# A fused attention and expert kernel: the work beside the attention scores is put into other units of each pair of heads

## The chip, the cores and the metric

The kernel runs on one core of a Trainium2 chip. The metric is the device time of one execution in microseconds (us), lower is better. The core has engines that run side by side, each through its own list of instructions in order: TensorE (PE in the profile, its weight loads PEld), VectorE (DVE), ScalarE (ACT), GpSimd (POOL), and SyncE (SP), which here only issues transfers (DMAs). An instruction that waits holds up everything behind it on its engine.

## The reference, cut to what matters

Three layers follow one another. The first is attention on 2 batches, 8 heads, 768 positions and 64 features per head, in which a query sees only the keys that fall into the same hash bucket; the second sends 1536 tokens to 8 experts; the third is a gated feed-forward layer with three matrices of 512 x 1536, 512 x 1536 and 1536 x 512.

```python
q_bits = (np.einsum('bhsd,dk->bhsk', q, proj) > 0)      # 6 bits a position; k_bits alike
mask = q_bucket[:, :, :, None] == k_bucket[:, :, None, :]
scores = np.where(mask, scale * np.matmul(q, k.transpose(0, 1, 3, 2)), -1e9)
attn = softmax(scores)
out = np.matmul(attn, v)
...                                                     # the experts: token to expert by greedy choice
x = silu(xn @ w_gate) * (xn @ w_val) @ w_out            # the third layer
```

The matrices of the third layer arrive as 64-bit floats, shown to the kernel as 64-bit integers (the "wide weights"). They are needed as 32-bit floats only hundreds of microseconds later, and are converted while the attention runs.

## The kernel before, in words

The attention takes the heads in 8 pairs (two heads of one batch). A pair has 12 **units**: 6 blocks of 128 queries by 2 heads. So there are 96 units, and the place of a unit in its pair runs from 0 to 11. In unit u the program writes down, in this order: the exponentials of unit u+1 (`expo`, L350, ScalarE); the six transposes of unit u (`transp`, L361, TensorE), whose two halves are copied out of the accumulator memory (PSUM), one by VectorE (L365) and one by ScalarE (L363), or both by ScalarE at places 0, 4 and 8; the scores of unit u+2 (`scores`, L336 and L339, TensorE) and their row minimum and exponent scale on VectorE (L341 to L343); the combination of a finished block (`comb`, L395, and L420 on VectorE) in even units, the reciprocals (L404, L405, VectorE) in odd ones; a part of the product with the values (`pv`, L380, TensorE); and then what is in `fill` for this unit. The transposes, the combination and the preparation share three PSUM buffers called m, in turn: a transpose waits until the buffer of three uses ago has been copied out.

Two kinds of work are in `fill`, put there by tables of unit numbers.

**Preparation of the next pair.** For the keys and then the queries, in two halves each, `prep_t` transposes on TensorE (L278), copies to SBUF on ScalarE (L282, L284) and splits into a high and a low part on GpSimd (L285, L286). After the second half `prep_d` issues six transfers on SyncE that stack the parts (L310 to L312). Two `prep_p` steps compute hash bits (six matmuls L294, then L297 on VectorE into the tile sg), and `prep_s` issues four transfers of sg (L320) into the stacked operands s_k and s_q. Then `load_pair` issues the loads of the pair after that (L98). `SLOTS` gives the places: keys at -1 and 0, queries at 1 and 3, `prep_p` at 5 and 6, and with the second of these `prep_s`. The first matmul of the next pair that needs what `prep_s` moves is L339 in unit 10 of the pair.

**Conversion of the wide weights.** 36 pieces of 128 x 512. For each, `conv_load` (L242, SyncE) is due five units ahead of `conv`, and `conv_store` (L263, SyncE) three units behind it. `conv` is one ScalarE instruction (L250), two VectorE instructions from SBUF to SBUF (L253, L254) and four GpSimd instructions (L255 to L258). The unit of piece n is 5 + 12n/5, rounded down, so that a pair has five pieces, spread over all its units (places 0, 2, 5, 7 and 9 in most pairs). A piece's load buffer is one of three, its sg buffer one of two, its ha buffer one of four.

Within a unit the preparation stands ahead of the conversion, and a piece's store ahead of the load of a later piece. The order of every engine is fixed by this writing order (`manual_schedule`): nothing is moved afterwards.

Of the kernel before, what the change touches and what calls it, by code (L numbers as in the profile page):

```python
# [23 lines left out]
BIG = 2.0 ** 30  # L24
ACT_EVAC = 1
SLOTS1 = (0, 0, 4, 5, 5, 6)
CONV = 5
SLOTS = (-1, 0, 1, 3, 5, 6)
WSTEP = (4, 7, 9, 10, 10, 13, 15, 16)
POOL_LO = (0, 1, 4, 5, 7)  # L30
DVE_HI = (0, 4)
# [15 lines left out]
def lsh_attention__moe__swiglu_kernel(ctx, tc, q, k, v, proj, m_wg, m_w1, m_w2,  # L47
# [8 lines left out]
    TPB = S // 128  # L56
# [5 lines left out]
    NPAIR = B * HP  # L62
# [164 lines left out]
    convs = []  # L227
    for src, dst in ((f_wg, wg_d), (f_wv, wv_d), (f_wo, wo_d)):
        n = src.shape[0] * src.shape[1] // (128 * 512)
# [281 lines left out]
    def at(u, f, *a):  # L511
        fill.setdefault(u, []).append((f, a))

    for p in range(1, NPAIR):
        u0 = (p - 1) * TPB * 2
        slots = iter(SLOTS if p > 1 else SLOTS1)
        for nm in "kq":
            for half in range(2):
                n = u0 + next(slots)
                at(n, prep_t, p, nm, half)  # L520
            at(n, prep_d, p, nm)
        for half in range(2):
            n = u0 + next(slots)
            at(n, prep_p, p, half)
        at(n, prep_s, p)
        if p + 1 < NPAIR:
            at(n + 1, load_pair, p + 1)
    for n in range(len(convs)):
        u = CONV + n * 12 // 5
        at(u - 5, conv_load, n)  # L530
        at(u, conv, n)
        at(u + 3, conv_store, n)
    for i in range(8):
# [779 lines left out]
```

## Time and profile before

| | |
|---|---|
| median of 3 runs | 816.4 us (815.01 to 816.46) |
| the profiled execution's own time | 814.53 us |
| its span, first to last instruction | 812.7 us |
| TensorE busy in the span | 761.3 us (94%) |
| VectorE, ScalarE, GpSimd busy in the span | 513.7, 398.0, 328.6 us |
| mean granted TensorE clock | 0.967 of full speed |
| the 96 units | from 22.1 us to 298.9 us |

Times in the rows are counted from the start of the span. "Busy" of TensorE includes matmuls that overlap one another, so 94% does not say that only 6% can be saved. The attention is read pair by pair: a stretch runs from the first transpose (L361) of a pair's unit 0 to that of the next pair. A bracket at the end of a timeline row is the idle time of that engine ahead of the instruction and what ended it. Behind the attention come the choice of the experts, the experts and the feed-forward layer, which the change does not touch.

### The profile page before, as it was taken

What the parts mean: (1) busy time and instruction counts of PE and PEld (TensorE: products, weight loads), DVE (VectorE), ACT (ScalarE), POOL (GpSimd) and SP (SyncE); (2) the same over time, 40 slices, a digit from 0 to 9 for tenths busy, and PEclk for the clock granted to TensorE, in tenths of its full rate; (3) what the DMA queues carried; (4) which work ended last, traced back from release to release, by engine and by line L of the source; (5) the groups of instructions that cost most, each with busy time, mean ns of one, the idle gap of its engine ahead of it and who ended that gap; (6) DMA issues with size and microseconds to landing.
All of it is one profiled execution on the core that took longest, in us unless ns stands there. A gap on an engine that the chain in (4) does not pass through costs nothing.

```text
span 812.7 us, 14759 instructions
## 1 busy us (share of the span) xinstructions
PE 761.3 (94%) x5317; PEld 685.2 (84%) x5317; DVE 513.7 (63%) x1342; ACT 398.0 (49%) x863; POOL 328.6 (40%) x309
## 2 busy tenths in 40 slices
PE   7999999999989983698999999999999999999997
PEld 3788777787878863498999999999999999999996
DVE  7788786889878878467787887766422332233222
ACT  3677765676766762265676776644211221121111
POOL 3278786877868720586767660000100010001001
PEclk8999999999999995699999999999999999999999
DMA  3578897989879612377777834363200110001001
GB/s 79 175 206 217 258 248 208 271 253 278 213 233 268 192 34 78 96 226 226 244 255 241 261 102 156 117 195 117 78 1 1 40 39 1 1 1 40 1 1 39
DMA packets 89770, 115.58 MB, mean 142 GB/s; under 512 B 22124, under 2 KB 68188, under 8 KB 89692
## 3 DMA queue, kind: packets, MB, share of 16 engines
q1 hardware_dynamic: 87612, 108.28, 44.8%
q0 software_dynamic: 1920, 6.29, 2.1%
q8 instruction: 44, 0.72, 0.4%
q14 instruction: 34, 0.28, 0.1%
q10 hardware_dynamic: 160, 0.00, 0.0%
HBM read 77.62 MB, written 18.87 MB: 119 GB/s over the span
## 4 chain that ended last, share of the span: by engine, by line
PE 37%; issue 18%; POOL 1%; DVE 1%; ACT 1%; POOLq 0%; ACTq 0%; DVEq 0%
PE pg L1194 6%; PE pv L1194 6%; PE py L1029 6%; PE po L1222 6%; PE ph L1005 6%; PE py L1031 3%; PE ph L1007 3%; POOL out_dram L1230 1%; PE ph L983 1%; PE py L1101 0%; DVE wl L218 0%; PE px L1061 0%; PE px L1084 0%; ACT bt L1015 0%; DVE yn L1091 0%
## 5 line engine op out<-in xcount | busy, mean ns | idle before, releaser
L1230 POOL DMA_INDIRECT out_dram<-ot,oi x12 | 11.7, 974 | 307.8 <-DVE ot L1228 306.2
L350 ACT ACTIVATE pr<-sc,rs 128x768 f32<-128x768 f32 x96 | 94.9, 989 | 50.4 <-DVE rs L343 31.6
L341 DVE TENSOR_REDUCE rs<-sc 128x1 f32<-128x768 f32 x96 | 91.5, 953 | 34.7 <-PE sc L339 34.2
L218 POOL TENSOR_TENSOR wl<-wr,wh 128x1024 fp32r<-128x1024 f32 x39 | 95.0, 2446 | 44.0 <-PE ph L983 20.9
L1203 DVE TENSOR_TENSOR a<-sg,pg 128x384 f32<-128x384 f32 x48 | 26.6, 553 | 103.1 <-ACT sg L1201 103.1
L361 PE MATMUL m<-ident,pr 128*128 128x128 f32 x576 | 83.4, 281 | 3.1 <-ACT pt L363 2.5
L380 PE MATMUL xo<-pt,ld_v 128*64 128x128 f32 x1128 | 82.9, 282 | 0.0
L1005 PE MATMUL ph<-xg,wh 128*128 128x384 f32 x256 | 75.3, 363 | 3.8 <-DVE ht L1022 3.1
L1029 PE MATMUL py<-ht,wh 128*128 128x384 f32 x256 | 76.7, 364 | 0.0
L361 PEld LDWEIGHTS m<-ident,pr 128*128 128x128 f32 x576 | 63.8, 141 | 15.1 <-issue 7.4
L380 PEld LDWEIGHTS xo<-pt,ld_v 128*64 128x64 f32 x1128 | 60.0, 137 | 18.6 <-issue 11.9
L1201 ACT ACTIVATE sg<-pg 128x384 f32<-128x384 f32 x48 | 23.5, 490 | 105.8 <-PE pg L1194 105.7
L1207 ACT ACTIVATE ah<-a 128x384 fp32r<-128x384 f32 x48 | 25.2, 525 | 99.3 <-DVE a L1204 99.3
L1194 PE MATMUL pg<-xh,gl 128*128 128x384 f32 x192 | 64.6, 336 | 0.0
L1194 PE MATMUL pg<-xl,gh 128*128 128x384 f32 x192 | 64.5, 336 | 0.0
L1194 PE MATMUL pg<-xh,gh 128*128 128x384 f32 x192 | 64.5, 336 | 0.0
L1194 PE MATMUL pv<-xh,vl 128*128 128x384 f32 x192 | 64.4, 335 | 0.0
L1194 PE MATMUL pv<-xl,vh 128*128 128x384 f32 x192 | 64.4, 335 | 0.0
L1194 PE MATMUL pv<-xh,vh 128*128 128x384 f32 x192 | 64.4, 335 | 0.0
L1031 PE MATMUL py<-ht,wl 128*128 128x192 f32 x256 | 63.7, 253 | 0.0
L215 ACT ACTIVATE wh<-wr 128x1024 fp32r<-128x1024 f32 x50 | 51.2, 1054 | 14.2 <-PE py L1029 11.4
L339 PE MATMUL sc<-s_k,s_q 82*128 82x384 f32 x192 | 49.9, 341 | 8.7 <-DMA s_q<-sg 8.7
(252 smaller groups left out, 1952.4 us busy)
## 6 DMA issues: line engine op xcount, KB each, us to landing
wr<-in_moe_w_dram SPq DMA_DIRECT2D x64, 512.0 KB, 4.7
w<-in_moe_w_gate_dram SPq DMA_DIRECT2D x12, 512.0 KB, 6.4
w<-in_moe_w_val_dram SPq DMA_DIRECT2D x12, 512.0 KB, 5.7
w<-in_moe_w_out_dram SPq DMA_DIRECT2D x12, 512.0 KB, 5.3
s_k<-nh_k SPq DMA_DIRECT2D x28, 192.0 KB, 3.4
s_q<-nh_q SPq DMA_DIRECT2D x28, 192.0 KB, 4.2
ld_v<-in_v_dram SPq DMA_DIRECT2D x8, 384.0 KB, 6.2
wg_d<-ha SPq DMA_DIRECT2D x12, 256.0 KB, 5.5
```

The costliest lines, as they stand in the source:

```text
L215: nc.scalar.activation(WH[i], WR[i], AF.Copy)
L218: (nc.gpsimd if pool else nc.vector).tensor_tensor(WL[i], WR.pop(i), WH[i], op=OP.subtract)
L339: nc.tensor.matmul(ps[:, n, :HALF], q2[:64 + NS, h, qs], k2[:64 + NS, h, n * HALF:(n + 1) * HALF], start=False, stop=True)
L341: nc.vector.tensor_reduce(rs[:, h, 0:1], ps[:, :, :HALF], axis=AX.XY, op=OP.min)
L350: nc.scalar.activation(pt, ps[:, :, :HALF], AF.Exp, scale=rs[:, h, 1:2], bias=rs[:, h, 2:3], accum_out=rs[:, h, 3:4])
L361: nc.tensor.transpose(t[:, i, :], pt[:, c * 128:(c + 1) * 128], ident)
L380: nc.tensor.matmul(xo[64 * h:64 * h + 64], vt[:, h, chunk(p, c), :], a[h][:, c, :], start=(c == 0), stop=(c == TPB - 1))
L1005: hi = lambda: nc.tensor.matmul(ph[:, :2 * CAP], wh[:, d], xg[:, d].rearrange("p a b -> p (a b)"), start=(d == 0), stop=(d == KD - 1), ski ...
L1029: hi = lambda: nc.tensor.matmul(py[d][:, :2 * CAP], wh[:, ds], ht[:, f].rearrange("p a b -> p (a b)"), start=(f == 0), stop=(f == KF - 1), ...
L1031: lo = lambda: nc.tensor.matmul(py[d][:, :CAP], wl[:, ds], ht[:, f, 0], start=False, stop=False, skip_group_check=True)
L1194: nc.tensor.matmul(t[:, :TJ], a[:, d, :], b_[:, d, :], start=(n == 0), stop=(n == 3 * KD - 1))
L1222: nc.tensor.matmul(PO[j][t], a[:, ts], b_, start=(f == 0 and n == 0), stop=(f == KG - 1 and n == 2))
```

## The change

The places of both kinds of work are changed; no instruction is added or taken away, apart from waits.

```diff
-CONV = 5
-SLOTS = (-1, 0, 1, 3, 5, 6)
+CONV1 = (6, 8, 9, 11)
+CONV5 = (3, 5, 6, 8, 9)
+CONV4 = (3, 5, 7, 9)
+CONVN = (0, 2, 4, 6, 8)
+SLOTS = (-1, 0, 1, 2, 4, 5)
...
-    for n in range(len(convs)):
-        u = CONV + n * 12 // 5
-        at(u - 5, conv_load, n)
+
+    turns = [CONV1] + [CONV5] * 3 + [CONV4] * (NPAIR - 5) + [CONVN]
+    units = [w * TPB * 2 + u for w, t in enumerate(turns) for u in t]
+    assert len(units) == len(convs)
+    for n, u in enumerate(units):
+        at(max(u - 5, units[n - 3] + 1 if n > 2 else 0), conv_load, n)
         at(u, conv, n)
         at(u + 3, conv_store, n)
```

The second half of the queries is prepared at place 2 instead of 3, and `prep_p` stands at 4 and 5 instead of 5 and 6. Pieces are converted at places 6, 8, 9, 11 of the first pair, 3, 5, 6, 8, 9 of pairs 2 to 4, 3, 5, 7, 9 of pairs 5 to 7, and 0, 2, 4, 6, 8 of the last pair (4 + 15 + 12 + 5 = 36). A load is no earlier than one unit behind the piece whose buffer it takes. Lines behind the tables are 3 higher in the new kernel (L253 becomes L256), those behind the loop 6 higher.

On GpSimd, this is the second pair of heads, from the second half of the keys on, in the kernel before (nh and nl are the high and low parts, ha a piece that is converted):

```order
L285 CAST nh_k<-nr_k 128x384
L286 TENSOR_TENSOR nl_k<-nr_k,nh_k 128x384
L255 TENSOR_SCALAR ha<-ha 128x512
L256 TENSOR_TENSOR ha<-ha,eight 128x512
L257 TENSOR_TENSOR ha<-ha,lr 128x512
L258 TENSOR_TENSOR ha<-ha,sg 128x512
L285 CAST nh_q<-nr_q 128x384
L286 TENSOR_TENSOR nl_q<-nr_q,nh_q 128x384
```

The same place in the new kernel:

```order
L288 CAST nh_k<-nr_k 128x384
L289 TENSOR_TENSOR nl_k<-nr_k,nh_k 128x384
L288 CAST nh_q<-nr_q 128x384
L289 TENSOR_TENSOR nl_q<-nr_q,nh_q 128x384
L425 COPY lp<-xs 128x6x16
L288 CAST nh_q<-nr_q 128x384
L289 TENSOR_TENSOR nl_q<-nr_q,nh_q 128x384
L258 TENSOR_SCALAR ha<-ha 128x512
```

In the kernel before one piece stands ahead of each half of the queries (the second follows in the same way); in the new one both halves stand ahead of the pieces.

On SyncE, this is the second pair behind the last stacking transfer of the queries, in the kernel before (wg_d is the store of a piece, w the load of one, sg the hash bits):

```order
L312 DMA s_q<-nl_q 64x2x384
L263 DMA wg_d<-ha 128x512
L242 DMA w_1046<-in_moe_w_gate_dram 128x512
L263 DMA wg_d<-ha 128x512
L320 DMA s_k<-sg 18x2x384 x2
L320 DMA s_q<-sg 18x2x384 x2
```

The same place in the new kernel, and what follows to the next two pieces:

```order
L315 DMA s_q<-nl_q 64x2x384
L266 DMA wg_d<-ha 128x512
L245 DMA w_1054<-in_moe_w_gate_dram 128x512
L323 DMA s_k<-sg 18x2x384 x2
L323 DMA s_q<-sg 18x2x384 x2
L101 DMA ld_k<-in_k_dram 128x2x384
L101 DMA ld_q<-in_q_dram 128x2x384
L101 DMA ld_v<-in_v_dram 128x2x384
L266 DMA wg_d<-ha 128x512
L245 DMA w_1160<-in_moe_w_gate_dram 128x512
```

One store that waits for a piece no longer stands ahead of the sg transfers; the load w_1160, of the piece of place 9, stands behind them and behind the next pair's loads.

On VectorE, this is the third pair in the new kernel, where the pieces of places 8 and 9 follow each other (in the kernel before at least two units' copies and minima stand between two pieces):

```order
L423 TENSOR_TENSOR xs<-m,ri 128x144
L256 TENSOR_SCALAR ha<-w_1592 128x512
L257 TENSOR_SCALAR sg<-w_1592 128x512
L368 COPY pt<-m 128x384
L344 TENSOR_REDUCE rs<-sc 128x1
L345 TENSOR_SCALAR rs<-rs 128x1
L346 TENSOR_SCALAR rs<-rs 128x1
L407 TENSOR_SCALAR ri<-rs 128x1 x2
L408 RECIPROCAL ri<-ri 128x2
L256 TENSOR_SCALAR ha<-w_1700 128x512
L257 TENSOR_SCALAR sg<-w_1700 128x512
L368 COPY pt<-m 128x384
```

The copy and the minimum that the next units wait for (L368, L344) stand behind each piece's two instructions.

## Rows read from the trace of the kernel before

**Rows 1.** Busy time by pair, pairs 2 to 8 (length, then each engine, clock, DMA).
```profile
56.59:91.66 35.07, 33.16 (x302) 28.14 (x301) 28.16 (x83) 24.46 (x55) 28.35 (x30) 1.00 0.83 232
91.66:129.72 38.06, 34.77 (x302) 29.60 (x301) 28.18 (x83) 24.59 (x55) 27.66 (x29) 0.96 0.90 261
129.72:164.69 34.97, 33.23 (x303) 28.18 (x301) 29.07 (x91) 24.49 (x55) 27.72 (x29) 1.00 0.82 227
164.69:199.62 34.93, 33.82 (x303) 28.13 (x302) 30.13 (x94) 25.10 (x56) 27.71 (x28) 1.00 0.89 258
199.62:236.35 36.73, 33.27 (x301) 28.16 (x301) 28.96 (x84) 24.08 (x53) 27.67 (x29) 1.00 0.86 250
236.35:269.68 33.33, 32.82 (x299) 27.75 (x297) 27.76 (x81) 24.22 (x54) 26.96 (x29) 1.00 0.85 239
269.68:298.87 29.19, 29.19 (x295) 24.84 (x293) 23.67 (x86) 21.17 (x47) 14.11 (x14) 1.00 0.26 84
```

**Rows 2.** Waits in the first 320 us (who, on whom: total, times, longest).
```profile
PE sc L339 <- DMA s_q<-sg: 8.7, 4, 3.0
```

**Rows 3.** The timeline of TensorE, units 10 of pairs 2 and 3.
```profile
87.38 0.59 PE L339 MATMUL sc<-s_k,s_q 82*128 82x384 f32 x2 [1.47 <-DMA s_q<-sg]
...
123.87 0.59 PE L339 MATMUL sc<-s_k,s_q 82*128 82x384 f32 x2 [2.87 <-DMA s_q<-sg]
```

**Rows 4.** Busy time in the stretch behind the second wait of rows 3.
```profile
124.80:128.20 3.40, 3.40 (x21) 3.07 (x20) 1.70 (x5) 1.57 (x3) 0.89 (x1) 0.50 1.05 402
```

**Rows 5.** The timelines of ScalarE and GpSimd, pair 2, second half of the queries.
```profile
67.53 0.49 ACT L282 ACTIVATE nr_q<-m 128x384 f32<-128x384 f32 x1 [0.19 <-PE m L278]
...
72.59 0.50 POOL L285 CAST nh_q<-nr_q 128x384 fp32r<-128x384 f32 x1
```

**Rows 6.** The timeline of SyncE, pair 2, the sg transfers and the next load.
```profile
80.32 1.70 SPq L320 DMA_DIRECT2D s_k<-sg  x2
82.08 1.60 SPq L320 DMA_DIRECT2D s_q<-sg  x2
...
85.31 0.41 SPq L242 DMA_DIRECT2D w<-in_moe_w_gate_dram  x1
```

**Rows 7.** Busy time by unit: an even, an odd, and unit 10 of pair 7.
```profile
79.82:82.38 2.56, 2.56 (x26) 2.24 (x25) 2.45 (x9) 2.44 (x6) 1.15 (x2) 1.00 0.92 194
82.38:84.69 2.31, 2.31 (x24) 1.89 (x23) 1.76 (x6) 1.59 (x4) 2.15 (x3) 1.00 0.75 291
264.49:267.37 2.88, 2.79 (x26) 2.18 (x24) 2.81 (x10) 2.20 (x5) 2.42 (x3) 1.00 0.89 265
```

**Rows 8.** The timeline of TensorE, pair 2, unit 5.
```profile
70.41 0.93 PE L361 MATMUL m<-ident,pr 128*128 128x128 f32 x6 [0.44 <-ACT pt L363]
```

**Rows 9.** The timeline of VectorE, pair 2, places 3 and 6.
```profile
65.09 1.43 DVE L253 TENSOR_SCALAR ha<-w 128x512 int32<-128x512 int32 x1
66.44 0.72 DVE L254 TENSOR_SCALAR sg<-w 128x512 int32<-128x512 int32 x1
...
74.73 0.42 DVE L253 TENSOR_SCALAR ha<-w 128x512 int32<-128x512 int32 x1
...
77.03 0.30 DVE L420 TENSOR_TENSOR xs<-m,ri 128x144 f32<-128x144 f32 x1
```

**Rows 10.** The timeline of GpSimd beside these.
```profile
64.95 1.27 POOL L258 TENSOR_TENSOR ha<-ha,sg 128x512 int32<-128x512 int32 x1
66.17 0.71 POOL L285 CAST nh_q<-nr_q 128x384 fp32r<-128x384 f32 x1
...
77.15 1.28 POOL L257 TENSOR_TENSOR ha<-ha,lr 128x512 int32<-128x512 int32 x1
78.52 1.28 POOL L258 TENSOR_TENSOR ha<-ha,sg 128x512 int32<-128x512 int32 x1
```

**Rows 11.** The timeline of ScalarE, pair 2, place 4.
```profile
68.89 0.99 ACT L350 ACTIVATE pr<-sc,rs 128x768 f32<-128x768 f32 x1 [0.87 <-DVE ri L404]
```

**Rows 12.** DMA issues on the page (KB each, median us from issue to landing).
```profile
w<-in_moe_w_val_dram SPq DMA_DIRECT2D x12, 512.0 KB, 5.7
```

## The prediction

> **What bounds the kernel now.** I read the busy time pair by pair first. TensorE is busy for 32.82 of 33.33 us (98%) in pair 7, the shortest, and the 12 units of pairs 2 to 7 are of equal work, yet they take from 33.33 to 38.06 us [rows 1]. So TensorE sets the pace, and the difference is waits. The view of waits names one: the scores' matmul L339 stood idle for the transfer of sg four times, 8.7 us in all, 3.0 at most [rows 2]. It is the first matmul of the next pair, in unit 10; pair 2 lost 1.47 us there, pair 3 2.87 [rows 3]. Behind the latter the granted clock is 0.50 for 3.40 us, the lower of its two levels (1.2 and 2.4 GHz) [rows 4]. Pair 3 is 2.99 us longer than pair 2 [rows 1], of which 1.40 is the longer wait; the other 1.6 us I put to the clock.
>
> Why sg is late is read from the timelines. ScalarE began to copy the last quarter of the queries at 67.53, and GpSimd began to split it at 72.59, 5.1 us later [rows 5]: pieces of weights stand ahead of it on GpSimd (first two order lists). That puts `prep_d` late on SyncE, and two stores of pieces stand ahead of the sg transfers, which began at 80.32 and took 3.36 us to issue [rows 6].
>
> **What the change removes.** Both halves of the queries now pass GpSimd ahead of the pieces. `prep_p` ends a unit sooner and sg is written at the start of unit 6. From the first sg issue to the matmul it took 87.38 - 80.32 = 7.1 us in pair 2 [rows 3, 6]. From unit 6 to L339 in unit 10 lie two even and two odd units, 2 x 2.56 + 2 x 2.31 = 9.7 us [rows 7], plus about 1 us of unit 10, less about 1 us until sg is written. So some 2.6 us are left over: the wait goes in all pairs, though a queue that is as full as behind pair 3's wait (DMA share 1.05 [rows 4]) eats part of that. Next in line there is TensorE itself.
>
> What a pair takes without waits: pair 7 has no long one. Its unit 10 is 2.88 us where an even unit has 2.56 [rows 7], and its unit 5 starts after the same short wait that I show for pair 2, 0.44 us [rows 8]; 33.33 - 0.32 - 0.44 = 32.6 us. The order of preparation changes, not its work, so 32.6 stands for the new pair too.
>
> **What the change adds.** No instruction is new, but pieces now follow each other in neighbouring units: 5 and 6, 8 and 9 in pairs 2 to 4, and 8 and 9 in pair 1. VectorE's two instructions of a piece read and write SBUF, and they take longer when GpSimd is at work on the piece before. At place 3 of pair 2, L253 took 1.43 us and L254 0.72; at place 6, with GpSimd idle, L253 took 0.42 [rows 9]. The long L253 ends at 66.52, 0.30 behind GpSimd's L258 (66.22), and L254 ends at 67.16, 0.28 behind GpSimd's next instruction (66.88) [rows 9, 10]. So VectorE waited out the instruction that GpSimd was in, and then the next one: 2.07 us from 65.09 to 67.16, against some 0.75 for a free pair of instructions, an extra of 1.3. There are six such pieces, one in each of pairs 2 to 7. Behind it the row minimum was late, the exponential began at 68.89 after an idle 0.87 us [rows 11], the copy out of PSUM behind that, and TensorE's next transposes stood idle for 0.44 [rows 8]. So about 0.9 of the 1.3 is absorbed.
>
> The Trainium skill, page "SBUF — State Buffer", section "Who interferes with whom", says that VectorE in a two-port mode and GpSimd share one port pair as an exclusive lock: whoever issues first holds it for the whole instruction, and the other is blocked entirely. This trace agrees (1.43 against 0.42 us). The rule speaks against this change, which puts VectorE's and GpSimd's halves of neighbouring pieces side by side; where the two merely shared bandwidth, the first rival below would hold.
>
> Now place 6 of pairs 2 to 4. The piece of place 5 stands as it stood in pair 2: L253 at 74.73, GpSimd's L257 from 77.15 to 78.43, L258 from 78.52 to 79.80 [rows 9, 10]. VectorE reaches the next piece right behind L420 (77.03 [rows 9]), by my reading at about 77.25. L257 has then begun 0.1 us earlier, so L253 waits it out, and L254 waits out L258, which L253 delays by 0.2 as it delayed the cast (0.71 [rows 10] against 0.50 [rows 5]). L254 ends at 79.80 + 0.2 + 0.28 = 80.28: 3.0 us, an extra of 2.3. Absorbed are 0.9, less about 0.5 because unit 7 has no transposes of the preparation as unit 3 had, and because the piece comes later in it. That leaves 1.8 to 2.2 us of TensorE idle; I take 2.1. Place 9 has the same geometry: it is reached one unit behind the piece of place 8, and its L254 can't end before that piece's L258, 79.80 - 74.73 = 5.1 us behind L253 of the first. I take 2.1 again. From both sides: nothing, if all is absorbed, to 3.0, if nothing is. The piece of place 8 meets only the rest of L258, which is absorbed.
>
> Pieces two units apart (4.87 us) meet only the last tenths of L258, which ends 5.07 us behind L253. That holds for pairs 5 to 7 and for pair 8.
>
> **The sum**, against the pairs of [rows 1]:
> - pairs 5 to 7: 3 x 32.6 = 97.8 instead of 34.93 + 36.73 + 33.33 = 104.99: -7.2
> - pairs 2 to 4: 97.8 + 6 x 2.1 = 110.4 instead of 35.07 + 38.06 + 34.97 = 108.10: +2.3
> - pair 1: one such neighbour, with GpSimd nearly through when place 8 comes: +1.8 (0 to 3.0)
> - pair 8: five pieces instead of three, every second unit. VectorE has 23.67 us of work in 29.19 [rows 1], so two more fit, but the last now stands at place 8, near the end: +0.4 (0 to 1)
>
> Together -2.7 us. The profiled execution took 814.53 us (1.8 around its span), so it would take 811.8; it lies 1.9 under the median of 816.4, from which I predict 813.7. Nothing behind the attention moves: the converted weights are read hundreds of us later.
>
> **The rivals.** *The neighbours cost little.* VectorE is busy some 28 of 33 us in a pair [rows 1], and if it catches up as after today's blocked piece, each neighbour costs about 0.5: seven cost 3.5 instead of 14.4, less 10.9. But then a late load shows. The piece of place 9 is loaded behind the sg transfers and the next pair's loads: 85.31 - 80.32 = 5.0 us behind the first of them [rows 6], and lands 5.7 later [rows 12], with the 1 us for sg 11.7 us into unit 6, where its turn comes after 9.7. Of these 2.0 us ScalarE's queue absorbs about half, since the exponential stands behind the piece: 3 x 1.0 back. Time: 813.7 - 10.9 + 3.0 = 805.8. In my forecast that load hides under the stall of place 6.
>
> *VectorE comes first at place 6.* 0.1 us decides. If L253 passes ahead of L257, then L254 waits out L257 alone and ends 1.3 us sooner: 3 x 1.3 = 3.9 less, 809.8. Against it: GpSimd is then one L258 behind when place 8 comes, and part of it returns.
>
> *The clock falls* (the slower side). Seven stalls of about 2 us are new, and each that drops the clock as in pair 3 costs 1.6 more. From the second drop on the kernel is slower than before; with four it takes 813.7 + 6.4 = 820.1. For it: 2.87 us were enough once [rows 3, 4]. Against it: the longest wait, 3.0 us in pair 6 [rows 2], left the pair's clock at 1.00, as 1.47 did in pair 2 [rows 1].
>
> *The change does not do what it says*: sg lands late all the same, since the transfers share full queues. Then pairs 5 to 7 keep their waits: 813.7 + 7.2 = 820.9. The 2.6 us left over speak against it.
>
> **Chances.** Forecast 0.42, cheap neighbours 0.22, VectorE first 0.13, clock 0.15, sg still late 0.04, smaller losses 0.04. The forecast's own range is 811 to 818: the neighbours' price by 0.3 each way, pair 1 and pair 8 by their bounds, and a drop or two. The whole range, 804 to 821, takes in the first rival and four drops. A change of less than 0.2% (1.6 us) can't be told from none. Of the forecast's 0.42 I give 0.23 to faster, 0.13 to no change and 0.06 to slower; with the rivals faster 0.58, same 0.13, slower 0.29.
>
> **What would show it.** Right: no idle time of L339 on sg in unit 10; pairs 5 to 7 at 32 to 33 us each; L256 of the new kernel (L253 here) at 1 us or more at places 6 and 9 of pairs 2 to 4, and idle time of TensorE at the transposes of units 8 and 11 behind VectorE's copy, about 2 us each; pairs 2 to 4 at 36 to 38 us. Wrong: pairs 2 to 4 at 33 to 34 us, L256 at its 0.42, or a clock of 0.50 in more than one pair.

## The result, and the profile after

The changed kernel took 827.45 us (median of 4 runs, 825.28 to 830.74) beside 816.43 for the kernel before in the same comparison: a ratio of 1.0137, 95% interval 1.0095 to 1.0179. It is slower by 1.4%. The forecast was 813.7, so the sign is wrong, and the time lies 6.5 us above the upper end of the range. The profiled execution took 830.74 us, the longest of the four, and has a span of 828.9 us at a mean clock of 0.958, so sizes read from it lie above those of the median. Its line numbers are three higher inside the attention than those of before (L256 is the old L253).

Busy time by pair, pairs 1 to 8 of the changed kernel, in the columns of [rows 1]:

```profile
22.63:58.77 36.14, 33.54 (x286) 27.87 (x284) 29.50 (x74) 23.52 (x52) 17.69 (x19) 1.00 0.71 213
58.77:102.93 44.16, 35.90 (x302) 30.10 (x301) 31.21 (x89) 25.60 (x57) 33.43 (x35) 0.94 0.70 204
102.93:144.98 42.05, 35.92 (x301) 30.66 (x301) 29.77 (x81) 24.64 (x54) 27.95 (x29) 0.91 0.73 206
144.98:185.33 40.35, 35.97 (x301) 30.44 (x301) 30.31 (x89) 24.62 (x54) 27.94 (x29) 0.92 0.81 228
185.33:220.04 34.71, 33.85 (x302) 28.53 (x302) 28.20 (x87) 24.55 (x54) 23.32 (x24) 0.99 0.80 227
220.04:254.55 34.51, 32.94 (x300) 28.23 (x301) 27.04 (x82) 23.55 (x52) 22.96 (x25) 1.00 0.80 228
254.55:287.36 32.81, 32.43 (x299) 27.87 (x297) 25.89 (x79) 23.68 (x53) 23.14 (x26) 1.00 0.83 231
287.36:316.84 29.48, 29.26 (x295) 24.84 (x293) 24.99 (x90) 22.24 (x49) 23.00 (x22) 1.00 0.38 128
```

The loss is in pairs 2 to 4: 126.56 us together, where [rows 1] have 108.10 and the forecast had 110.4. TensorE is idle there for 18.77 of 126.56 us, and its busy time itself has grown, because the clock is below 1.00 in all three. Pairs 5 to 7 take 102.03 (before 104.99, forecast 97.8).

The view of waits of the same kernel, 22 to 320 us (who, on whom: total, times, longest), shows a new kind of wait:

```profile
ACT lr L253 <- DMA w<-in_moe_w_gate_dram: 8.4, 3, 4.6
ACT lr L253 <- DMA w<-in_moe_w_val_dram: 7.9, 2, 4.9
DVE ha L256 <- DMA w<-in_moe_w_val_dram: 6.9, 2, 3.9
DVE ha L256 <- DMA w<-in_moe_w_gate_dram: 6.4, 3, 4.1
PE m L364 <- ACT pr L353: 11.8, 5, 4.3
```

The wait of [rows 2] has no row any more: no matmul waits for sg. In its place, ScalarE and VectorE stand idle at the first instruction of a piece because the piece's wide weights have not landed, and TensorE's transposes wait for the exponential (L353) that is queued behind that instruction.

ScalarE's three longest are at place 9: 4.60, 4.86 and 3.09 us in pairs 2, 3 and 4. Here is the one in pair 3. First ScalarE, VectorE and TensorE in their timelines (start, duration, engine, line; idle time before and its releaser in brackets):

```profile
133.22 0.28 ACT L388 ACTIVATE xt<-xo 128x128 f32<-128x128 f32 x1 [0.18 <-PE xo L383]
138.36 0.67 ACT L253 ACTIVATE lr<-w 128x512 int32<-128x512 uint32 x1 [4.86 <-DMA w<-in_moe_w_val_dram]
138.93 0.98 ACT L353 ACTIVATE pr<-sc,rs 128x768 f32<-128x768 f32 x1
...
138.37 0.43 DVE L256 TENSOR_SCALAR ha<-w 128x512 int32<-128x512 int32 x1 [3.94 <-DMA w<-in_moe_w_val_dram]
...
140.05 1.54 PE L364 MATMUL m<-ident,pr 128*128 128x128 f32 x6 [4.31 <-ACT pr L353]
```

L253 waits 4.86 us, the exponential follows at 138.93, and six transposes that take 0.87 us elsewhere take 1.54. Why they take longer is in the busy time of the stretch from the end of ScalarE's wait on (column PEclk):

```profile
138.25:145.05 6.80, 5.00 (x26) 4.23 (x27) 4.66 (x14) 3.76 (x8) 4.30 (x4) 0.50 0.13 52
```

The granted clock is 0.50, its lower level, for 6.80 us, twice as long as in [rows 4]. It fell 1.8 us before the transposes began, while TensorE was idle. Now SyncE, whose order says when that load was issued:

```profile
123.03 1.78 SPq L323 DMA_DIRECT2D s_k<-sg  x2
124.86 1.59 SPq L323 DMA_DIRECT2D s_q<-sg  x2
126.50 0.47 SPq L205 DMA_DIRECT2D wr<-in_moe_w_dram  x1
127.41 1.22 SPq L101 DMA_DIRECT2D ld_k<-in_k_dram  x1
128.68 0.47 SPq L101 DMA_DIRECT2D ld_q<-in_q_dram  x1
130.28 0.37 SPq L101 DMA_DIRECT2D ld_v<-in_v_dram  x1
130.88 0.34 SPq L266 DMA_DIRECT2D wg_d<-ha  x1
131.37 0.34 SPq L245 DMA_DIRECT2D w<-in_moe_w_val_dram  x1
```

The load of place 9 is the last row, issued at 131.37 behind four transfers of sg, a load of expert weights, the three loads of the next pair and a store. It landed 138.36 - 131.37 = 7.0 us later.

The step at place 6 itself went as forecast. VectorE and TensorE, pair 3:

```profile
124.63 1.49 DVE L256 TENSOR_SCALAR ha<-w 128x512 int32<-128x512 int32 x1
126.02 1.53 DVE L257 TENSOR_SCALAR sg<-w 128x512 int32<-128x512 int32 x1
...
128.16 0.48 PE L398 MATMUL m<-cb,xt 128*128 128x144 f32 x2 [0.47 <-DVE pt L368]
130.80 0.87 PE L364 MATMUL m<-ident,pr 128*128 128x128 f32 x6 [1.35 <-ACT pt L366]
```

The neighbour's two instructions take 2.92 us together (124.63 to 127.55), where the free pair of run 4 below takes 0.75, and TensorE is idle for 0.47 + 1.35 us behind them: unit 8 takes 4.68 us (126.12 to 130.80), where [rows 7] have 2.56.

### The profile page after: what moved, and what is told of

The parts are those of the page before. It is cut to its first block, busy times and chain, and to the rows that moved or that the text cites. A ratio compares the mean times of both kernels' runs of the same rounds, so it can differ in the third digit from the quotient of the medians.

```text
span 828.9 us, 14759 instructions
## 1 busy us (share of the span) xinstructions
PE 768.0 (93%) x5317; PEld 690.6 (83%) x5317; DVE 517.4 (62%) x1342; ACT 397.9 (48%) x863; POOL 329.4 (40%) x309
## 4 chain that ended last, share of the span: by engine, by line
PE 35%; issue 18%; DVE 1%; POOL 1%; ACT 1%; POOLq 0%; DVEq 0%
PE pg L1200 6%; PE pv L1200 6%; PE po L1228 6%; PE py L1035 6%; PE ph L1011 5%; PE py L1037 3%; PE ph L1013 2%; POOL out_dram L1236 1%; PE ph L989 1%; PE py L1107 0%; DVE wl L221 0%; PE px L1067 0%; PE px L1090 0%; ACT wh L218 0%; ACT sq L1053 0%
## 5 line engine op out<-in xcount | busy, mean ns | idle before, releaser
L1236 POOL DMA_INDIRECT out_dram<-ot,oi x12 | 11.7, 974 | 307.7 <-DVE ot L1234 306.2
L353 ACT ACTIVATE pr<-sc,rs 128x768 f32<-128x768 f32 x96 | 95.0, 990 | 38.8 <-DVE rs L346 20.2
L344 DVE TENSOR_REDUCE rs<-sc 128x1 f32<-128x768 f32 x96 | 91.5, 953 | 30.8 <-PE sc L342 30.5
L364 PE MATMUL m<-ident,pr 128*128 128x128 f32 x576 | 85.4, 286 | 21.7 <-ACT pr L353 11.8
L364 PEld LDWEIGHTS m<-ident,pr 128*128 128x128 f32 x576 | 66.0, 145 | 33.7 <-ACT pt L366 13.0
L383 PE MATMUL xo<-pt,ld_v 128*64 128x128 f32 x1128 | 84.7, 287 | 0.0
L339 PE MATMUL sc<-s_k,s_q 128*128 128x384 f32 x192 | 58.7, 388 | 0.0
L366 ACT ACTIVATE pt<-m 128x384 f32<-128x384 f32 x120 | 55.9, 489 | 4.6 <-PE m L364 4.3
```

The costliest lines, as they stand in the source:

```text
L339: nc.tensor.matmul(ps[:, n, :HALF], q1[:, h, qs], k1[:, h, n * HALF:(n + 1) * HALF], start=True, stop=False)
L344: nc.vector.tensor_reduce(rs[:, h, 0:1], ps[:, :, :HALF], axis=AX.XY, op=OP.min)
L353: nc.scalar.activation(pt, ps[:, :, :HALF], AF.Exp, scale=rs[:, h, 1:2], bias=rs[:, h, 2:3], accum_out=rs[:, h, 3:4])
L364: nc.tensor.transpose(t[:, i, :], pt[:, c * 128:(c + 1) * 128], ident)
L366: nc.scalar.activation(o[:, 3 * half:3 * half + 3, :], t, AF.Copy)
L383: nc.tensor.matmul(xo[64 * h:64 * h + 64], vt[:, h, chunk(p, c), :], a[h][:, c, :], start=(c == 0), stop=(c == TPB - 1))
```

## The experiments

All times are medians beside the kernel before in the same comparison; the first four share one comparison (before 813.61 us), the next four a second (815.26) and the last four a third (815.34). "Theory C" is that SyncE's one order makes a piece's transfers late; it was formed after the second run.

**1. One more load buffer.** The changed kernel, with the load of a piece allowed one piece sooner:

```diff
-        w = cv.tile([128, 512], I64, name="w64", bufs=3)
+        w = cv.tile([128, 512], I64, name="w64", bufs=4)
-        at(max(u - 5, units[n - 3] + 1 if n > 2 else 0), conv_load, n)
+        at(max(u - 5, units[n - 4] + 1 if n > 3 else 0), conv_load, n)
```

> The new kernel with four load buffers for the pieces instead of three, and each load due one unit behind the piece of four ago: the load of place 9 is then issued ahead of the sg transfers. Theory A (the late loads cost most: they hold ScalarE's queue, the wait lets the clock fall): no wait of L253 or L256 on a load in pairs 2 to 4, about 36.8 us each of these pairs (two neighbours at 2.1 us), clock drops gone; some 809 us. Theory B (the neighbours on VectorE and GpSimd cost most, the late load only coincides): pairs 2 to 4 stay at 40 us or more, above 820 us.

Measured: 826.6 us (822.77 to 827.33), ratio 1.0127, 1.0069 to 1.0186. Pairs 2 to 4 take 42.56, 39.97 and 40.89 us. The waits of place 9 for its load are gone, and another stands in the same place. VectorE and SyncE in pair 3:

```profile
136.92 0.43 DVE L256 TENSOR_SCALAR ha<-w 128x512 int32<-128x512 int32 x1 [3.84 <-DMA wg_d<-ha]
...
131.24 1.40 SPq L266 DMA_DIRECT2D wg_d<-ha  x3
```

L256 writes a buffer of ha that must first be stored, and the store of the piece four before it is issued at 131.24, behind the same sg transfers and the same loads. So the wait went from one buffer of the pieces to the next, and the time hardly moved. The run does not speak against the late transfers; it shows that they reach the engines in two ways, through a load and through a store.

**2. No neighbours.** The changed kernel with its pieces two units apart wherever it can be:

```diff
-CONV1 = (6, 8, 9, 11)
-CONV5 = (3, 5, 6, 8, 9)
+CONV1 = (5, 7, 9, 11)
+CONV5 = (3, 5, 7, 9, 11)
```

> The new kernel with the pieces two units apart everywhere: places 5, 7, 9, 11 in pair 1 and 3, 5, 7, 9, 11 in pairs 2 to 4; three load buffers as in the new kernel. Both theories: neighbours gone, and the load behind the sg transfers belongs to place 11, two units later than place 9, so it lands in time: pairs 2 to 4 at 32.6 to 33.5 us each, the whole at 797 to 803 us. If pairs 2 to 4 stay above 36 us, neither holds, and the preparation ahead of the pieces costs something that is not seen yet.

Measured: 826.92 us (826.4 to 830.11), ratio 1.0156, 1.0099 to 1.0213. No VectorE instruction of a piece is held up for 1 us any more (the longest L256 takes 0.79), pair 1 is back at 34.47, and yet pairs 2 to 5 take 39.39, 38.97, 39.45 and 40.83: ScalarE waits 3.8, 4.1, 3.6 and 4.1 us for the load of place 7. That load stands behind the stacking of the queries. Both theories had expected 797 to 803 us, and both failed: with the neighbours gone another late load takes their place, so a late load is not bound to place 9. What the neighbours cost by themselves this run can't say; run 11 does.

**3. The preparation alone.** The kernel before with the new places of the preparation and the old ones of the pieces:

```diff
-SLOTS = (-1, 0, 1, 3, 5, 6)
+SLOTS = (-1, 0, 1, 2, 4, 5)
```

> The kernel before with the new places of the preparation alone, pieces as before. On GpSimd the second half of the queries then stands ahead of the piece of place 2, so sg is out about a unit and a half earlier. Theory (the wait for sg is what the early preparation is worth, the pieces' new places are what costs): no idle time of L339 on sg, pairs 2 to 7 at 32.6 to 33.4 us, 800 to 804 us. Rival (the preparation can't be early unless the pieces leave the first half): sg still late in pairs 2 to 6, within 3 us of the kernel before.

Measured: 804.5 us (803.84 to 805.0), ratio 0.987, 0.9819 to 0.9922. Pairs 2 to 4, busy time:

```profile
56.63:90.26 33.63, 33.06 (x302) 28.21 (x301) 27.87 (x83) 24.23 (x55) 27.71 (x30) 1.00 0.87 252
90.26:123.89 33.63, 33.07 (x302) 28.21 (x301) 27.88 (x83) 24.25 (x55) 27.66 (x30) 1.00 0.92 259
123.89:157.31 33.42, 32.91 (x302) 28.27 (x301) 28.86 (x90) 24.26 (x55) 27.55 (x30) 1.00 0.91 272
```

100.68 us instead of 108.10 [rows 1], at clock 1.00, with no wait for sg and none for a load; the whole lies 0.5 us above the expected range, and pair 5 still takes 35.06. This half of the change is a gain of 1.3%; all of the loss is in the other half or in the two together.

**4. A lighter GpSimd.** The kernel of the first run, where GpSimd leaves out three of the four instructions of the first piece of each neighbouring two in pairs 1 to 4:

```diff
+FIRSTS = (1, 5, 7, 10, 12, 15, 17)
...
+        if n not in FIRSTS:
             nc.gpsimd.tensor_tensor(ha, ha, eight.to_broadcast([128, 512]), op=OP.mult)
```

> As e1_four_load_buffers, but GpSimd leaves out three of its four instructions for the first piece of each neighbouring two (seven pieces, which are then stored unfinished), so that it is idle when VectorE comes with the second; VectorE and ScalarE do all they did. If VectorE is held up by GpSimd's instruction: the second pieces' L256 and L257 at 0.42 us, pairs 2 to 4 at 33 us each, some 11 us less than e1. If VectorE is simply short of time with two pieces in a row: within 3 us of e1.

Measured: 823.97 us (821.96 to 825.54), ratio 1.0112, 1.0056 to 1.0169. The neighbour of place 6 in pair 3, VectorE (the lines are one higher here):

```profile
119.65 0.42 DVE L257 TENSOR_SCALAR ha<-w 128x512 int32<-128x512 int32 x1
119.98 0.42 DVE L258 TENSOR_SCALAR sg<-w 128x512 int32<-128x512 int32 x1
```

0.42 each instead of 1.49 and 1.53, and unit 8 is back at 2.56 us. So it was GpSimd's work on the piece before that held them up. The Trainium skill, page "SBUF — State Buffer", section "Who interferes with whom", has the ports that VectorE and GpSimd share as an exclusive lock. The two traces agree (1.49 us beside GpSimd's instructions, 0.42 without them). But the wait for the store at place 9 stays (5.2 us in pair 2, 5.3 in pair 3), and the time falls by some 2.6 us only, where 11 were expected with GpSimd as the cause; the two intervals overlap, so this run does not price the neighbours.

**5. Buffers for both.** The kernel of the first run with six buffers of ha instead of four:

```diff
-        ha = cv.tile([128, 512], I32, name="ha", bufs=4)
+        ha = cv.tile([128, 512], I32, name="ha", bufs=6)
```

> The changed kernel with four load buffers (w64) and six result buffers (ha), so that neither a piece's load nor its VectorE work waits for a buffer that a late store or a late conversion holds. Theory C (SyncE issues in one order, and what a piece needs is issued behind the stacking and the next pair's loads): the waits of 3 to 5 us at place 9 and the stretches at clock 0.50 in pairs 2 to 4 go; the neighbours' blocked port stays (2.1 us at place 6, less at place 9), so pairs 2 to 4 take 36 to 37 us each, and the whole 811 to 817. Rival N (the neighbouring pieces themselves crowd VectorE and ScalarE, whatever the queue does): pairs 2 to 4 stay at 40 us or more and the time over 822.

Measured: 817.78 us (815.99 to 821.17), ratio 1.0031, 1.0007 to 1.0055. Pairs 2 to 4:

```profile
58.55:96.06 37.51, 33.88 (x303) 28.14 (x301) 32.75 (x85) 25.20 (x57) 32.54 (x35) 1.00 0.75 218
96.06:132.93 36.87, 33.11 (x303) 28.21 (x302) 31.47 (x82) 24.53 (x55) 28.01 (x30) 1.00 0.87 257
132.93:169.85 36.92, 33.39 (x303) 28.15 (x302) 31.82 (x89) 24.53 (x55) 28.07 (x30) 1.00 0.88 240
```

111.30 us, with the clock at 1.00: 15.3 less than in the changed kernel, and within 1 us of the forecast's 110.4. The places of the pieces are the same, so only the late transfers went. Of the 15.3 us, 107.79 - 100.38 = 7.4 are TensorE's busy time (the low clock) and 7.9 its idle time. These are the two profiled executions (830.74 and 815.99 us); the ratios of the medians, 1.0137 and 1.0031, put the two kernels only some 8.6 us apart.

**6. Buffers, and no neighbours.** The last kernel with the places of the second run:

```diff
-CONV1 = (6, 8, 9, 11)
-CONV5 = (3, 5, 6, 8, 9)
+CONV1 = (5, 7, 9, 11)
+CONV5 = (3, 5, 7, 9, 11)
```

> The buffers of the run before, and the pieces at places 3, 5, 7, 9 and 11 (first pair 5, 7, 9, 11), so that no two are neighbours. Theory C: neither a late load or store nor a blocked port is left, pairs 2 to 5 take 33 to 34 us each, no stretch at clock 0.50 in the attention, and the whole time is 800 to 806, as with the preparation alone. Rival D (the second half of a pair has no room for the pieces once SyncE is busy with the next pair's loads): places 5 and 7 still wait 3 us and more for a transfer, pairs 2 to 5 stay near 39 us and the time over 820.

Measured: 827.24 us (824.26 to 830.28), ratio 1.0124, 1.0071 to 1.0177. Theory C failed here as I had put it: buffers are plenty, and ScalarE waits 3.9, 4.4, 4.0 and 3.8 us for the load of place 7 in pairs 2 to 5. The rows of pair 3, GpSimd's last instruction of the piece of place 11 and its second copy of the next keys, SyncE's first stacking transfer and the load of place 7, and ScalarE's wait:

```profile
101.57 1.28 POOL L261 TENSOR_TENSOR ha<-ha,sg 128x512 int32<-128x512 int32 x1
102.80 0.50 POOL L288 CAST nh_k<-nr_k 128x384 fp32r<-128x384 f32 x1
...
103.33 0.65 SPq L313 DMA_DIRECT2D s_k<-nh_k  x1
...
118.23 0.38 SPq L245 DMA_DIRECT2D w<-in_moe_w_gate_dram  x1
...
123.77 0.68 ACT L253 ACTIVATE lr<-w 128x512 int32<-128x512 uint32 x1 [4.39 <-DMA w<-in_moe_w_gate_dram]
```

SyncE issues its first stacking transfer as soon as GpSimd has copied the second half of the keys, and from there on it issues one transfer after the other: 14.9 us lie between it and the load of place 7, filled with 12 stacking transfers, two stores, a load and two writes of results. GpSimd's copy came late because the piece of place 11 stands ahead of it. More buffers cannot help a load that stands behind the stacking by the order.

**7. The places alone.** The changed kernel with the old places of the preparation:

```diff
-SLOTS = (-1, 0, 1, 2, 4, 5)
+SLOTS = (-1, 0, 1, 3, 5, 6)
```

> The other half of the change alone: the pieces' new places and their loads' new times, with the preparation of the next pair where it was before (three load buffers, four result buffers). Theory C: the stacking of sg and the next pair's loads now stand one place later still, in front of the load of place 9, so the same waits come and the time is 824 to 834. Rival G (the new places cost only in company with GpSimd's and SyncE's earlier preparation): no wait over 1 us for a load, and 812 to 819.

Measured: 820.65 us (818.71 to 823.67), ratio 1.0057, 1.0032 to 1.0081. Below what theory C expected and just above its rival's range. The load of place 9 waits less (2.0, 1.8 and 1.5 us in pairs 2 to 4), and the order on SyncE says why: with `prep_s` at place 6 the loads of the next pair come at place 7, behind that load; in the changed kernel they come at place 6, ahead of it. Run 9 tries this alone. In pair 6 a matmul waits 2.96 us for sg again, as in the kernel before. So neither half is as slow as the two together: the earlier preparation pulled the next pair's loads in front of the load of place 9.

**8. The preparation alone, the pieces one place later.** The kernel of the third run with

```diff
-CONV = 5
+CONV = 6
```

> The preparation alone, as in the third run, with all pieces one place later (evenly spaced, from place 6 on instead of place 5). Theory C: the loads stay five units ahead and nothing waits for them, so 802 to 807, as the third run, with perhaps the one blocked piece in each pair moved or gone (0.3 to 0.9 us a pair). Rival P (the places of the even spacing were lucky against the new preparation): a load or a blocked port ends late in several pairs and the time is 810 or more.

Measured: 800.51 us (799.45 to 803.48), ratio 0.9817, 0.9765 to 0.987. Even a little below the range of theory C: pairs 2 to 7 take 32.41 to 34.47 us. The piece of place 3 still meets GpSimd (L253 takes 1.35 to 1.39 us in four of the pairs), and one load is late by 1.5 us.

**9. The next pair's loads one unit later.** The changed kernel, one line:

```diff
-            at(n + 1, load_pair, p + 1)
+            at(n + 2, load_pair, p + 1)
```

> The changed kernel with one line other: the loads of the pair after next (k, q and v) are issued one unit later in the order, at place 7 instead of place 6, and so behind the store of the piece of place 3 and the load of the piece of place 9 instead of ahead of them. Buffers, places and preparation as in the changed kernel. Theory C (SyncE's order alone makes that load and that store late): the load of place 9 is issued some 4 us sooner, its wait of 4.9, 4.6 and 3.1 us in pairs 2 to 4 falls to 1 us or less, the clock keeps its level there, and the neighbours' blocked port stays; pairs 2 to 4 take 36.5 to 38 us and the whole 815 to 820, as with more buffers. Rival B (the transfer is late because the DMA engines are full with the stacking, not because of when it is issued): pairs 2 to 4 stay at 40 us or more and the time over 823.

Measured: 818.56 us (816.87 to 820.68), ratio 1.0044, 1.0022 to 1.0066. SyncE in pair 3:

```profile
120.10 1.60 SPq L323 DMA_DIRECT2D s_q<-sg  x2
121.74 0.48 SPq L205 DMA_DIRECT2D wr<-in_moe_w_dram  x1
122.33 0.43 SPq L266 DMA_DIRECT2D wg_d<-ha  x1
122.87 0.37 SPq L245 DMA_DIRECT2D w<-in_moe_w_val_dram  x1
124.62 0.38 SPq L101 DMA_DIRECT2D ld_k<-in_k_dram  x1
```

The load of place 9 is now issued 4.65 us behind the first sg transfer (118.22) instead of 8.34, and ScalarE waits 0.7 us for it instead of 4.9. Pairs 3 and 4 take 36.87 and 36.88 us, as with all the buffers. Two things did not go as expected. Pair 2 keeps a wait of 3.0 us at place 9 and takes 40.21: its first sg transfer is issued only 6.23 us into unit 6 (83.19), where it is 1.70 in pair 3, because SyncE is still stacking. And in pair 4 the clock falls, at the neighbours' stall of place 6, with no load waited for. The transfers, the buffers and the places are those of the changed kernel; moving one group of issues in SyncE's order brought the loss from 1.4% to 0.4%, and the two intervals do not overlap. The rival, that the DMA engines were too full, would have left it at over 823.

**10. Shifted pieces and earlier loads.** The kernel of run 8 with four load buffers, six of ha, and

```diff
-        at(u - 5, conv_load, n)
+        at(max(u - 7, 0), conv_load, n)
```

> The version with the preparation alone and the pieces one place later, with four load buffers and six result buffers and each load seven units ahead instead of five. Theory C: the one wait left there (1.5 us for the load of place 8 in pair 3) goes, since that load now stands ahead of the stacking of q; 0 to 2 us less than that version, so 798 to 801. Rival: the loads, two units earlier, now stand ahead of the stacking or the sg transfers and make these late; 803 or more.

Measured: 799.03 us (798.74 to 799.12), ratio 0.9803, 0.977 to 0.9837. No wait for a load of wide weights is left in the attention. It is the fastest of all, 2% below the kernel before; from run 8 it can't be told apart, the intervals overlap.

**11. Buffers, and a lighter GpSimd.** The kernel of run 5 with the edit of run 4 (the same three instructions left out for the same pieces).

> The kernel with four load and six result buffers and the changed places, in which GpSimd leaves out three of its four instructions for the first piece of each neighbouring two in the pairs 1 to 4 (their results are not complete). With no transfer late any more, this prices the neighbours alone. If the blocked port is what is left: the second piece of the two takes 0.42 us on VectorE instead of up to 1.5, pair 1 goes back from 36.1 to 34.5, pairs 2 to 4 from 37 to 33.5 to 34.5 each, and the time from 817.8 to 806 to 810. If the neighbours cost by ScalarE's and VectorE's work itself: pairs 2 to 4 stay over 36 and the time over 814.

Measured: 810.17 us (807.19 to 813.49), ratio 0.994, 0.9916 to 0.9965. With no transfer very late, this prices the neighbours: 7.6 us less than run 5 for all seven. Pair 1 goes from 36.13 to 34.54, pair 3 from 36.87 to 32.98: 1.6 us for its one neighbour, and 3.9 for the two of pair 3. Pairs 2 and 4 (36.51 and 34.24) keep waits for loads, up to 2.3 and 0.5 us; pair 2 misses what was expected of it by 2 us.

**12. Spaced pieces, and GpSimd light at place 11.** The kernel of run 6 with

```diff
+FIRSTS = (3, 8, 13, 18)
...
+        if n not in FIRSTS:
```

in front of the same three instructions, which leaves them out for the piece of place 11 in pairs 1 to 4.

> The kernel with the buffers and the spaced pieces, in which GpSimd leaves out three of its four instructions for the piece of place 11 in the pairs 1 to 4 (their results are not complete). In that kernel the stacking of k began 1.3 units later than with the preparation alone, and the load of place 7, which stands behind the stacking of q, was issued two units later. Theory G (GpSimd's work for the piece of place 11 stands ahead of its second copy of k, and all of SyncE's queue begins later by that): the stacking of k begins 3 us sooner in the unit's terms, the wait of 3.2 to 4.4 us at place 7 falls below 1.5 us in pairs 2 to 5, these take 33.5 to 36 us, and the time falls from 827 to 806 to 814. Rival S (SyncE's own issues set it, whatever GpSimd does): the wait stays over 3 us, and the time over 820.

Measured: 806.77 us (803.31 to 808.0), ratio 0.9888, 0.9846 to 0.9929, 20 us less than run 6. The rows of pair 3 that answer to those of run 6:

```profile
94.66 0.51 POOL L290 CAST nh_k<-nr_k 128x384 fp32r<-128x384 f32 x1 [0.80 <-ACT nr_k L289]
...
95.19 0.65 SPq L315 DMA_DIRECT2D s_k<-nh_k  x1
...
109.08 1.15 SPq L246 DMA_DIRECT2D w<-in_moe_w_gate_dram  x1
...
114.39 0.67 ACT L254 ACTIVATE lr<-w 128x512 int32<-128x512 uint32 x1 [0.28 <-DMA w<-in_moe_w_gate_dram]
```

Counted from the start of the pair (95.81 in run 6, 90.86 here), the first stacking transfer goes from 7.5 to 4.3 us, the load of place 7 from 22.4 to 18.2, and the wait from 4.39 to 0.28. Pairs 2 to 5 take 33.26 to 34.69 us. So in these pairs the chain of causes is complete: GpSimd's piece in front of the copy, the copy in front of SyncE's stacking, the stacking in front of the load, the load in front of the exponential. Pair 6 is an exception: its load of place 7 is issued as early (18.2 us into the pair) but lands 8.2 us later instead of 5.3, ScalarE waits 3.2 us, and the pair takes 39.0 us at a clock of 0.91.

## Why the prediction was wrong

**Right: the wait for sg goes.** The row of [rows 2] is gone, and run 3 prices it: pairs 2 to 4 at 33.4 to 33.6 us.

**Right: the neighbours' price, where it can be read alone.** The forecast had 2.1 us for each. Run 11 against run 5 gives 3.9 for the two of pair 3, 1.95 each, and 1.6 for pair 1 (forecast 1.8; in the changed kernel itself pair 1 is 1.66 longer than before). Over all seven the medians differ by 7.6 us, not by the 14.4 of the forecast, partly because load waits take the neighbours' place in pairs 2 and 4. Pair 8 cost 0.3 (forecast 0.4).

**Too small: pairs 5 to 7.** They take 102.03 us, 4.2 above the 97.8. I had taken 32.6 from pair 7 for all three. Pair 5 has TensorE busy for 33.85 us, and had 33.82 before [rows 1, fourth row], so 32.6 could not hold there; and pair 6 has a load wait of 1.7 us. Only pair 7 (32.81) fits. The same 32.6 stands under pairs 2 to 4, where TensorE was busy for 33.16 us and more before [rows 1] and run 3 took 33.4 to 33.6. So it is partly luck that run 5 comes so near the forecast's 110.4: the base was 2.9 us too low (97.8 against 100.68), and over that base the six neighbours cost 10.6 us, not 12.6.

**Wrong, the step that failed: "In my forecast that load hides under the stall of place 6."** I had counted the load of place 9 as landing 11.7 us into unit 6 and its turn at 9.7 + 2.1 = 11.8, and so put its wait at nothing. In the changed kernel each part of that count came out longer (us; unit 6 begins at 77.55, 121.31 and 162.82):

| | forecast | pair 2 | pair 3 | pair 4 |
|---|---|---|---|---|
| start of unit 6 to the first sg transfer | 1.0 | 6.81 | 1.72 | 2.47 |
| from there to the issue of the load | 5.0 | 5.56 | 8.34 | 7.90 |
| from the issue to its landing | 5.7 | 6.39 | 6.99 | 6.50 |
| landed, from the start of unit 6 | 11.7 | 18.76 | 17.05 | 16.87 |
| its turn on ScalarE | 11.8 | 14.16 | 12.19 | 13.78 |
| ScalarE's wait | 0 | 4.60 | 4.86 | 3.09 |

In pairs 3 and 4 the largest term is the distance on SyncE, which I had copied from pair 2 of before [rows 6]. Of the 3.3 us that it grew by in pair 3, 1.4 are two transfers that stood behind the load in the old order and stand in front of it in the new one (the expert weights, 0.91, and a store, 0.49); the other 1.9 are the next pair's three loads, which stood in front in both, and which took SyncE 3.47 us instead of 1.59. In pair 2 it is the first term: SyncE was still stacking when unit 6 began. GpSimd's second copy of the keys, and the first sg transfer there:

```profile
66.33 0.52 POOL L288 CAST nh_k<-nr_k 128x384 fp32r<-128x384 f32 x1
...
84.36 1.72 SPq L323 DMA_DIRECT2D s_k<-sg  x2
```

That copy stands behind the piece of place 11 of pair 1, so the stacking began 8.1 us into pair 2 (66.88), against 4.7 into pair 3 (107.68). It is the chain that run 12 shows.

**Wrong with it: the clock.** That rival had 0.15 and 1.6 us for each drop. The clock fell in all of pairs 2 to 4, which the forecast itself had named as a sign of being wrong. It stood at 0.50 once in pair 2 (6.8 us), once in pair 3 (6.8) and twice around pair 4 (3.4 each). Three of the four go with the load waits, with TensorE idle for 4.16, 4.31 and 2.56 us. The first in pair 4 does not; TensorE and the busy time behind its stall at place 6:

```profile
172.32 1.52 PE L364 MATMUL m<-ident,pr 128*128 128x128 f32 x6 [1.35 <-ACT pt L366]
...
172.38:175.79 3.41, 3.41 (x18) 2.97 (x20) 2.70 (x6) 2.19 (x5) 2.88 (x4) 0.50 1.08 289
```

Here TensorE stood idle behind a neighbour only, as the rival had it. The drops cost 7.4 us in TensorE's busy time over three pairs (run 5), 2.5 a pair, because the low level lasts 6.8 us a pair here and not 3.4.

**The sum, mended.** Pairs 2 to 4: 110.4 forecast, 111.3 with the late transfers taken away (run 5), and 15.3 for the late transfers, half of it clock: 126.6. With pairs 5 to 7 (+4.2) that is 20.4 us. The profiled span is 18.9 above the forecast's (828.9 against 811.8 - 1.8 = 810.0); pairs 1 and 8 came out 0.2 lower, and what lies outside the attention takes back the remaining 1.3. This is the account of one execution, 3.3 us above the median; the medians leave some 8.6 us for the late transfers, not 15.3 (run 5).

**What stays open.** Why the same kind of load lands 5.3 us behind its issue in pair 3 of run 12 and 8.2 in pair 6 was not tried. Nor was what holds SyncE between the loads ld_q and ld_v in the changed kernel (129.15 to 130.28), nor why the stall of place 6 lets the clock fall in pair 4 and not in pairs 2 and 3.

## What to carry to other kernels

When work on an engine is packed together, write down the new order of the queue that feeds it and count what now stands in front of each transfer; a lead of five units in a table means little when the queue has 14.9 us of other issues in front of the load (run 6). A wait that more buffers remove can come back at the next buffer of the same chain, so give each of its buffers the same lead, or move what stands in front. And look at what side work stands in front of, not only at its spacing: here the pieces spread over all units of a pair (runs 3, 8 and 10) beat every other table, but the pieces two units apart from place 3 to 11 (runs 2 and 6) were as slow as the changed kernel. The earlier preparation by itself was worth 1.3%.

## What the runs showed of the hardware

With an idle time of TensorE of 4.31 us the granted clock stood at 0.50 for 6.80 us, from within the wait on, where it was 3.40 us behind one of 2.87 [rows 3, 4]. The length of the last idle time alone does not tell: behind the 1.35 us of place 6 the clock fell in pair 4 (3.41 us at 0.50) and stayed in pairs 2 and 3, and behind 3.00 us in pair 6 of the kernel before it stayed. A 512 KB load landed 7.0 us behind its issue when it was issued right behind the next pair's three loads, against a median of 5.7 [rows 12]; among all the runs' rows shown or told here it took 5.3 to 8.2. And a pair of VectorE instructions that meets GpSimd between two of its long ones loses time on both: 1.49 and 1.53 us against 0.42 each, all of which came back when GpSimd's three instructions were left out.
